# Reordering the first loads, with fewer warm-up matmuls, in a gated mix of memory attention and a GeGLU layer

## The chip, the core and the metric

The kernel runs on one core of a Trainium2 chip. Its engines are TensorE (PE: matmuls; PEld: the loads of their stationary operand), VectorE (DVE), ScalarE (ACT), GpSimd (POOL) and SyncE (SP), and each has a queue of its own that it works off in order. SyncE and ScalarE issue the DMAs. The metric is device time in microseconds (us) of one execution, the median of several. The profile is one further execution, taken by the hardware profiler; its times count from the first instruction, and lines such as L505 are lines of the kernel before.

## The reference

```
x = A_x                                               # 1 x 2048 x 512, bf16
g = sigmoid((x * gate_w).sum(-1, keepdims=True))
q, k, v = x @ wq, x @ wk, x @ wv                      # 32 heads of 16, 4 segments of 512
for s in range(4):
    p = softmax(q_s @ k_s.T * 16**-0.5 + mask)        # mask: ar[:, None] < ar[None, :]
    a_dot = p @ v_s
    a_mem = (phi(q_s) @ M) / (phi(q_s) @ z + 1e-6)
    o_s = sigmoid(beta) * a_mem + (1 - sigmoid(beta)) * a_dot
    M, z = M + phi(k_s).T @ v_s, z + phi(k_s).sum(rows)
a = concat(o) @ wo
b = (gelu(x @ w_gate) * (x @ w_up)) @ w_down          # 512 -> 1792 -> 512
return g * a + (1 - g) * b
```

Here phi(t) is t + 1 where t > 0 and exp(t) elsewhere. In the kernel the gate g is folded into factors, so that one accumulation per row tile holds both branches.

## The kernel before, in words

The four segments of 512 rows are worked one after another, but their tasks overlap. For a segment s, `prep` (L720) computes K, Q and V from the transposed input xT, `memory` (L826) the running M and z, `attention` (L860) the scores, their exponentials (ScalarE), masks (GpSimd) and value products; the gate, up and down matmuls of the GeGLU fill TensorE between the scores. Nearly all plain matmuls are recorded at L505 (128x128 stationary, up to 512 columns); the scores at L868 (four row tiles of 32) and the value products at L916 and L924 (column tiles) use the array in tiles.

Every piece of work is a task with a name. The order in which each engine works its tasks off is written out in `ORDER` (L41), one list for each engine; TensorE's pieces are named like `K0_1.2` (segment 0, tile 1, instruction 2 on). `schedule` (L240) goes through these lists with estimated durations and assigns the four PSUM banks; the constants `COLD` (L33: until when TensorE is taken to be at half speed) and `LANDING` (L37: when each early load is taken to have landed) enter it there (L281, L297). They issue nothing themselves. `Emitter` (L319) then writes each engine's stream, with a semaphore wait wherever a task reads what another engine or a DMA wrote.

The head of the program is what the change touches:

- ScalarE issues `wk` in two halves of 256 KB and then `wq` in two halves, and only then runs `tload` (L567), a one-column exponential that makes the table load happen early.
- SyncE issues the first segment's x in two halves of 256 rows (`x0_0`, `x0_1`, L572; they land in a part of hT[1]), then `wv` in two halves, half of `wg`, the second segment's x (transposing DMAs), `gate_w` (gwb), `beta` and the other half of `wg`.
- TensorE runs 11 warm-up matmuls on constants (L587: 512 columns, three of them 384), ten before and one behind the first transposes.
- Segment 0's x is transposed by TensorE (L599: x0t0a, x0t0b, x0t1 for the first half, x0t0, x0t1 for the second; eight transposes of 128 x 128 for each half) into PSUM, and copied out to xT by VectorE and ScalarE (x0ev..).
- The K projections of segment 0 (`proj_T`, L665) are cut into halves of 256 columns, one for each half of x0, each of four matmuls over the 128-row blocks kb. Matmul K0_t.j is block kb = j for the first half (j below 4) and kb = j - 4 for the second. `wk_of` (L675) says which load a block waits for: blocks 0 and 1 the first half of wk, blocks 2 and 3 the second.
- Q of segment 0 goes into the score banks X; V and the GeGLU gates into the four W banks.

The weights for up, down and out are loaded later, each behind the exponential of a given score group.

Of the kernel before, what the change touches and what calls it, by code (L numbers as in the profile page):

```python
# [32 lines left out]
COLD = 4.9  # L33
# [4 lines left out]
    "w_wk0": 4.8, "x0_0": 4.4, "w_wk1": 6.2, "x0_1": 5.8, "w_wq0": 8.2, "w_wv0": 7.4, "w_wq1": 10.1, "w_wv1": 8.9,  # L38
    "w_wg0": 11.5, "x1_0": 12.1, "w_gwb": 12.4, "x1_1": 13.0, "w_beta": 13.3, "x1_2": 13.8, "x1_3": 14.3,
# [3 lines left out]
        "warm0 warm1 warm2 warm3 warm4 warm5 warm6 warm7 warm8 warm9 x0t0a_0 x0t0b_0 x0t1_0 warm10 K0_0.0 K0_1.0 "  # L43
        "K0_2.0 K0_3.0 K0_0.1 K0_1.1 K0_2.1 K0_3.1 x0t0_1 x0t1_1 K0_0.2 K0_0.3 K0_2.2 K0_3.2 K0_2.3 K0_3.3 K0_1.2 "
        "K0_1.3 K0_1.4 K0_1.5 K0_1.6 K0_1.7 K0_3.4 K0_0.4 K0_0.5 K0_0.6 K0_0.7 K0_2.4 K0_3.5 Q0_1.0 K0_2.5 Q0_3.0 "
        "Q0_0.0 K0_2.6 K0_2.7 Q0_2.0 Q0_1.2 Q0_2.2 Q0_0.2 V0_1.0 Q0_3.2 V0_1.2 K0_3.6 V0_0.0 qk0_0A0 V0_3.0 "
        "K0_3.7 V0_3.2 V0_2.0 V0_0.2 V0_2.2 G1_1.0 qk0_0B0 G1_5.0 G0_4.0 G0_4.2 G0_5.0 G1_5.2 qk0_0L G0_8.0 "
        "G0_5.2 G0_8.2 G1_1.2 Q1_2.0 qk0_0A1 Q1_3.0 Q1_3.2 G0_3.0 G0_3.2 G1_2.0 qk0_0B1 G1_10.0 Q1_2.2 G1_10.2 "
        "G1_2.2 G1_11.0 G1_11.2 qk0_1A0 G0_1.0 G1_0.0 G0_1.2 G1_0.2 Q1_0.0 qk0_1B0 Q1_1.0 Q1_0.2 Q1_1.2 G1_9.0 "
        "G1_7.0 qk0_1A1 G1_9.2 K1_0.0 K1_0.2 G1_7.2 pv0_0_0 pv0_0_1 qk0_1B1 K1_1.0 G0_7.0 K1_1.2 G0_7.2 G0_9.0 "  # L50
        "G0_6.0 G0_9.2 qk0_2A0 G0_2.0 G0_6.2 K1_2.0 G0_2.2 K1_2.2 G0_10.0 qk0_2B0 G0_10.2 mz0 pv0_1_0 pv0_1_1 "
        "qk0_2L K1_3.0 G0_0.0 K1_3.2 V1_2.0 V1_0.0 qk0_2A1 G0_0.2 V1_2.2 G1_12.0 G1_12.2 V1_0.2 qk0_2B1 Q2_0.0 "
        "Q2_0.2 V1_3.0 G0_13.0 V1_3.2 qk0_3A0 G0_13.2 G1_6.0 G1_8.0 G1_8.2 G0_11.0 qk0_3B0 G0_11.2 G1_6.2 G1_3.0 "
        "G1_3.2 G1_4.0 qk0_3A1 G1_4.2 Q2_2.0 G0_12.0 G0_12.2 Q2_2.2 qk0_3B1 pv0_2_1 pv0_2_0 Q2_3.0 Q2_3.2 U0_1.0 "
        "G1_13.0 G1_13.2 V1_1.0 qk1_0A0 V1_1.2 U0_2.0 U0_1.2 U0_0.0 U0_0.2 U0_2.2 U0_3.0 U0_3.2 U0_4.0 U0_4.2 "
        "U0_9.0 U0_9.2 U0_7.0 U0_7.2 U0_10.0 U0_6.0 U0_10.2 U0_6.2 U0_8.0 U1_2.0 U0_8.2 U1_1.0 U1_2.2 U1_1.2 "
        "U1_5.0 U1_5.2 U1_7.0 U1_0.0 U1_0.2 U1_13.0 U1_13.2 num1_01.0 U1_7.2 U1_10.0 U1_10.2 pv0_3_1 pv0_3_0 "
        "qk1_0B0 U0_5.0 U0_5.2 U0_11.0 U1_6.0 U1_6.2 Q2_1.0 num1_00.0 qk1_0L U0_11.2 Q2_1.2 U1_11.0 U1_11.2 "
        "U0_13.0 qk1_0A1 D0_2.0 U0_12.0 U0_12.2 U0_13.2 D0_0.0 qk1_0B1 D0_0.2 D0_2.2 num1_02.0 D0_0.4 D0_0.6 "
        "U1_3.0 qk1_1A0 D0_0.8 D0_2.4 U1_3.2 U1_9.0 D0_2.6 U1_9.2 qk1_1B0 D0_2.8 D0_0.10 D0_0.12 D0_0.14 D0_0.16 "  # L60
        "num1_10.0 qk1_1A1 U1_8.0 U1_8.2 D0_2.10 D0_2.12 num1_11.0 D0_2.14 num1_12.0 qk1_1B1 U1_12.0 U1_12.2 "
        "D0_2.16 pv1_0_0 pv1_0_1 qk1_2A0 V2_3.0 K2_0.0 V2_3.2 K2_0.2 U1_4.0 qk1_2B0 U1_4.2 mz1 pv1_1_1 pv1_1_0 "
        "qk1_2L D0_1.0 D0_3.0 D0_3.2 D0_3.4 D0_1.2 qk1_2A1 D0_1.4 D0_1.6 D0_3.6 D0_1.8 D0_1.10 qk1_2B1 D0_1.12 "
        "V2_1.0 D0_1.14 K2_3.0 V2_1.2 qk1_3A0 D0_1.16 K2_3.2 K2_1.0 D0_3.8 K2_1.2 qk1_3B0 D0_3.10 D0_3.12 Q3_1.0 "
        "D0_3.14 Q3_1.2 qk1_3A1 V2_0.0 G2_0.0 K2_2.0 V2_0.2 K2_2.2 D0_3.16 qk1_3B1 pv1_2_0 pv1_2_1 G2_0.2 G2_1.0 "
        "G2_3.0 G2_1.2 G2_2.0 G2_3.2 G2_2.2 G2_4.0 G2_4.2 G2_6.0 G2_5.0 G2_5.2 G2_6.2 G2_7.0 G2_7.2 qk2_0A0 "
        "pv1_3_1 pv1_3_0 G2_8.0 G2_9.0 G2_8.2 G2_9.2 G2_11.0 G2_11.2 G2_10.0 G2_10.2 G2_12.0 G2_12.2 G2_13.0 "
        "G2_13.2 num2_00.0 U2_9.0 U2_9.2 U2_3.0 V2_2.0 D1_0.0 U2_3.2 V2_2.2 D1_0.2 D1_0.4 num2_01.0 D1_0.6 "
        "qk2_0B0 D1_0.8 U2_6.0 num2_02.0 D1_0.10 U2_6.2 U2_13.0 U2_13.2 qk2_0L D1_2.0 D1_0.12 Q3_0.0 Q3_0.2 "
        "D1_2.2 qk2_0A1 D1_2.4 U2_8.0 U2_8.2 D1_0.14 num2_11.0 D1_2.6 qk2_0B1 U2_10.0 D1_2.8 U2_10.2 D1_2.10 "  # L70
        "D1_0.16 num2_10.0 qk2_1A0 Q3_3.0 Q3_3.2 D1_2.12 D1_2.14 D1_2.16 num2_12.0 qk2_1B0 U2_0.0 U2_7.0 U2_0.2 "
        "Q3_2.0 U2_7.2 qk2_1A1 Q3_2.2 V3_0.0 V3_0.2 U2_4.0 U2_4.2 qk2_1B1 pv2_0_0 mz2 pv2_0_1 pv2_1_0 qk2_2A0 "
        "D1_1.0 D1_1.2 U2_11.0 U2_11.2 D1_1.4 qk2_2B0 U2_5.0 D1_1.6 D1_1.8 D1_1.10 pv2_1_1 qk2_2L D1_1.12 D1_1.14 "
        "U2_5.2 K3_3.0 K3_3.2 qk2_2A1 D1_3.0 D1_3.2 V3_2.0 D1_3.4 V3_2.2 qk2_2B1 D1_3.6 K3_2.0 K3_2.2 D1_1.16 "
        "K3_1.0 qk2_3A0 K3_1.2 D1_3.8 V3_1.0 D1_3.10 D1_3.12 qk2_3B0 U2_12.0 D1_3.14 D1_3.16 V3_1.2 U2_12.2 "
        "qk2_3A1 U2_1.0 V3_3.0 U2_1.2 pv2_2_0 pv2_2_1 qk2_3B1 V3_3.2 G3_0.0 G3_0.2 G3_1.0 K3_0.0 K3_0.2 G3_2.0 "
        "G3_2.2 G3_1.2 G3_5.0 G3_3.0 G3_3.2 G3_4.0 G3_4.2 G3_5.2 G3_7.0 G3_6.0 G3_6.2 G3_8.0 G3_7.2 G3_9.0 "
        "G3_10.0 G3_8.2 G3_9.2 G3_11.0 G3_10.2 G3_12.0 G3_11.2 G3_12.2 G3_13.0 G3_13.2 qk3_0A0 pv2_3_1 pv2_3_0 "
        "U3_9.0 U3_9.2 U2_2.0 U2_2.2 U3_8.0 U3_7.0 qk3_0B0 U3_5.0 U3_10.0 U3_8.2 U3_7.2 U3_5.2 qk3_0L U3_10.2 "
        "U3_3.0 U3_3.2 U3_4.0 D2_0.0 qk3_0A1 num3_01.0 U3_4.2 D2_0.2 D2_0.4 num3_00.0 D2_0.6 num3_02.0 qk3_0B1 "  # L80
        "D2_0.8 D2_0.10 D2_1.0 D2_1.2 U3_6.0 qk3_1A0 D2_0.12 U3_2.0 D2_0.14 U3_6.2 U3_2.2 qk3_1B0 D2_0.16 D2_1.4 "
        "U3_13.0 D2_1.6 D2_1.8 qk3_1A1 num3_11.0 num3_10.0 D2_1.10 D2_1.12 D2_1.14 U3_13.2 qk3_1B1 U3_1.0 "
        "num3_12.0 D2_1.16 U3_1.2 U3_0.0 qk3_2A0 pv3_0_0 pv3_0_1 U3_0.2 D2_3.0 qk3_2B0 D2_3.2 D2_3.4 pv3_1_1 "
        "pv3_1_0 qk3_2L D2_3.6 D2_3.8 D2_3.10 D2_2.0 D2_3.12 qk3_2A1 D2_3.14 D2_2.2 D2_2.4 D2_2.6 D2_3.16 qk3_2B1 "
        "D3_1.0 D2_2.8 D2_2.10 U3_12.0 U3_12.2 qk3_3A0 D3_1.2 D2_2.12 U3_11.0 D3_1.4 D2_2.14 qk3_3B0 U3_11.2 "
        "D3_0.0 D3_1.6 D2_2.16 D3_0.2 qk3_3A1 pv3_2_0 pv3_2_1 D3_1.8 D3_0.4 qk3_3B1 D3_0.6 D3_1.10 D3_0.8 D3_1.12 "
        "D3_0.10 D3_3w1.0 pv3_3_0 pv3_3_1 D3_3w0.0 D3_0.12 D3_2.0 D3_2.2 D3_0.14 D3_2.4 D3_2.6 D3_1.14 D3_0.16 "
        "D3_1.16 D3_3w1.4 D3_3w1.8 D3_3w0.4 D3_3w1.12 D3_3a1.0 D3_2.8 D3_2.10 D3_2.12 D3_2.14 D3_2.16 D3_3w0.8 "
        "D3_3w0.12 D3_3a0.0 "),
    "act": (  # L90
        "w_wk0 w_wk1 w_wq0 w_wq1 tload x0ev0b_0 x0ev1_0 K0_1ev K0_0even pke0_0 Q0_1ev Q0_0ev Q0_3ev gexp Vev0_1 "
        "exp0_0A0 Vev0_3 Vev0_0 exp0_0B0 gsum0_1 exp0_0L Gev1_1 exp0_0A1 gexs0 Gev0_3 exp0_0B1 pke0_1 exp0_1A0 "
        "Gev1_0 exp0_1B0 Q1_0ev exp0_1A1 pqe1_0 Gev1_9 exp0_1B1 K1_1ev Gev0_9 exp0_2A0 K1_2ev exp0_2B0 pqe1_1 "
        "exp0_2L K1_3ev exp0_2A1 Gev1_12 exp0_2B1 gsum1_0 exp0_3A0 Vev1_3 exp0_3B0 Gev1_3 exp0_3A1 Gev0_12 gexs1 "
        "exp0_3B1 gelu0_0 Gev1_13 gelu0_2 gelu0_6 gelu0_10 gelu1_0 gelu1_7 exp1_0A0 kl1_01 exp1_0B0 exp1_0L "
        "Q2_1ev exp1_0A1 exp1_0B1 pke1_0 exp1_1A0 pke1_1 exp1_1B0 fin0_0 exp1_1A1 pqe2_0 exp1_1B1 fin0_2 exp1_2A0 "
        "K2_0ev exp1_2B0 pqe2_1 exp1_2L exp1_2A1 exp1_2B1 gsum2_0 exp1_3A0 gsum2_2 exp1_3B0 gexs2 Q3_1ev exp1_3A1 "
        "K2_2ev exp1_3B1 gelu2_0 gelu2_1 gelu2_2 gelu2_3 gelu2_4 gelu2_5 gelu2_6 gelu2_7 gelu2_8 gelu2_9 gelu2_10 "
        "gelu2_11 gelu2_12 gelu2_13 exp2_0A0 exp2_0B0 pke2_0 exp2_0L exp2_0A1 pke2_1 exp2_0B1 fin1_0 exp2_1A0 "
        "Q3_3ev exp2_1B0 fin1_2 exp2_1A1 exp2_1B1 Vev3_0 exp2_2A0 exp2_2B0 pqe3_0 exp2_2L exp2_2A1 K3_3ev "  # L100
        "exp2_2B1 exp2_3A0 exp2_3B0 gsum3_3 gexs3 exp2_3A1 pqe3_1 exp2_3B1 gelu3_0 gelu3_1 gelu3_2 gelu3_3 "
        "gelu3_4 gelu3_5 gelu3_6 gelu3_7 gelu3_8 gelu3_9 gelu3_10 gelu3_11 gelu3_12 gelu3_13 exp3_0A0 exp3_0B0 "
        "exp3_0L exp3_0A1 exp3_0B1 exp3_1A0 exp3_1B0 exp3_1A1 exp3_1B1 exp3_2A0 exp3_2B0 exp3_2L exp3_2A1 "
        "exp3_2B1 fin2_3 exp3_3A0 exp3_3B0 exp3_3A1 exp3_3B1 fin3_0 fin3_1 fin3_2 fin3_30 "),
# [1079 lines left out]
```

## Time and profile before

| | us |
|---|---|
| median of 3 runs (266.59 to 267.54) | 267.41 |
| the profiled execution | 267.31 |
| its span, first to last instruction | 265.6 |
| TensorE busy in the span | 261.7 |
| ScalarE busy | 209.8 |
| VectorE busy | 201.2 |
| GpSimd busy | 109.0 |
| first warm-up matmul starts | 0.84 |
| first transpose of x0 starts | 5.10 |
| first K matmul starts | 5.88 |
| first scores start | 14.57 |

"Busy" counts an instruction from its start to its end. Matmuls are pipelined, so a busy TensorE may still have holes: what shows them is the distance from one matmul's start to the next. The time between the span and the measured time lies outside the first and last instruction. The chain that ended last is followed back from the end of the span, at each step to the work that released it. A landing time is counted from the start of a DMA's issue.

### The profile page before, as it was taken

To read this page: it belongs to the slowest core of one execution; us is meant where nothing else is said; L and a number is where in the kernel's file an instruction comes from. 1 tells how busy PE (TensorE), PEld (TensorE's weight loads), DVE (VectorE), ACT (ScalarE), POOL (GpSimd) and SP (SyncE) were. 2 spreads that over 40 slices of the span, in tenths; PEclk is the share of its full clock that TensorE was granted. 3 is DMA by queue.
4 is the path that set the end of the run, shared out by engine and by line. 5 is a ranking of instruction groups with operands and counts; after the bars stand their busy time and mean duration, and the time that the engine had idled before them with its cause. 6 is when DMAs were issued, how large, how long until landed. Compare 5 with 4: busy or idle time off the path is not lost.

```text
span 265.6 us, 7154 instructions
## 1 busy us (share of the span) xinstructions
PE 261.7 (99%) x3021; PEld 119.5 (45%) x3021; DVE 201.2 (76%) x399; ACT 209.8 (79%) x182; POOL 109.0 (41%) x256
## 2 busy tenths in 40 slices
PE   8999999999999999999999999999999999999995
PEld 3644345434445444534444444544444444444452
DVE  0589988989889897858987875886895965892650
ACT  3589998999997899979948798887977767768611
POOL 8305857075400483372560137416184056245400
PEclk9999999999999999999999999999999999999999
DMA  6960357905102443750000246200000202201002
GB/s 213 308 173 0 63 133 131 225 17 158 61 0 47 136 62 81 151 70 22 0 2 2 47 110 106 83 2 22 1 2 0 46 0 62 62 0 42 22 12 69
DMA packets 32752, 18.23 MB, mean 69 GB/s; under 512 B 20560, under 2 KB 32720, under 8 KB 32720
## 3 DMA queue, kind: packets, MB, share of 16 engines
q1 hardware_dynamic: 31632, 16.73, 27.4%
q10 hardware_dynamic: 1088, 1.05, 1.2%
q8 instruction: 23, 0.38, 0.6%
q14 instruction: 9, 0.07, 0.1%
HBM read 9.84 MB, written 2.10 MB: 45 GB/s over the span
## 4 chain that ended last, share of the span: by engine, by line
PE 96%; DMA 2%; ACT 1%; issue 0%; ACTq 0%
PE psW L505 76%; PE psXALL L868 9%; PE psW L916 6%; PE psXALL L505 3%; DMA hT<-in_A_x_dram 2%; PE psW L924 1%; PE psW L836 1%; ACT pt L874 1%; PE psXALL L599 0%; ACT ost L1044 0%; PE psW L590 0%; ACTq L401 0%
## 5 line engine op out<-in xcount | busy, mean ns | idle before, releaser
L874 ACT ACTIVATE pt<-psXALL 128x2048 bf16<-128x2048 f32 x64 | 120.1, 1876 | 23.3 <-PE psXALL L868 21.2
L877 POOL TENSOR_SCALAR_AFFINE_SELECT pt<-pt 128x256 bf16<-128x256 bf16 x128 | 57.5, 460 | 72.1 <-ACT pt L874 67.2
L505 PE MATMUL psW<-xT,wu 128*128 128x512 bf16 x224 | 56.0, 380 | 0.0
L505 PE MATMUL psW<-wd,hT 128*128 128x512 bf16 x210 | 55.2, 380 | 0.0
L505 PE MATMUL psW<-xT,wg 128*128 128x512 bf16 x224 | 53.4, 380 | 0.0
L877 POOL TENSOR_SCALAR_AFFINE_SELECT ptl<-ptl 128x512 bf16<-128x512 bf16 x32 | 23.9, 746 | 65.5 <-ACT ptl L874 63.8
L1015 DVE TENSOR_TENSOR hT<-psW,hT 128x512 bf16<-128x512 f32 x56 | 37.0, 682 | 14.3 <-PE psW L505 13.9
L505 PEld LDWEIGHTS psW<-xT,wg 128*128 128x128 bf16 x224 | 20.8, 98 | 25.7 <-issue 1.9
L505 PEld LDWEIGHTS psW<-xT,wu 128*128 128x128 bf16 x224 | 20.5, 98 | 24.7 <-issue 1.5
L930 DVE STREAM_TRANSPOSE tb<-psW 128x512 f32<-128x512 f32 x32 | 21.7, 701 | 9.0 <-PE psW L924 8.9
L505 PEld LDWEIGHTS psW<-wd,hT 128*128 128x128 bf16 x210 | 18.6, 98 | 21.6 <-issue 3.2
L868 PE MATMUL psXALL<-qT,kpad 32*128 32x320 bf16 (+3 forms) x512 | 25.4, 273 | 0.1
L999 ACT ACTIVATE hT<-psW 128x512 bf16<-128x512 f32 x28 | 15.4, 596 | 7.2 <-PE psW L505 7.1
L916 PE MATMUL psW<-pt,vaug 128*17 128x192 bf16 (+3 forms) x512 | 18.8, 273 | 0.0
L868 PEld LDWEIGHTS psXALL<-qT,kpad 32*128 32x128 bf16 x512 | 7.6, 92 | 23.9 <-ACT pt L874 14.2
L779 POOL COPY exsT<-exs 32x4 f32<-32x4 f32 x64 | 16.7, 261 | 3.7
L505 PE MATMUL psW<-wv,xT 128*128 128x512 bf16 x64 | 18.2, 380 | 0.0
L505 PE MATMUL psW<-xT,wk 128*128 128x512 bf16 (+1 forms) x80 | 18.0, 337 | 0.0
L874 ACT ACTIVATE ptl<-psXALL 128x2048 bf16<-128x2048 f32 x8 | 15.0, 1876 | 3.4 <-PE psXALL L868 3.4
L505 PE MATMUL psW<-wo,oT 128*128 128x512 bf16 x60 | 16.5, 381 | 0.0
L522 DVE CAST hT<-psW 128x512 bf16<-128x512 f32 x19 | 12.6, 682 | 2.2 <-PE psW L505 2.1
L916 PEld LDWEIGHTS psW<-pt,vaug 128*17 128x17 bf16 x512 | 10.6, 91 | 7.9 <-issue 3.2
(102 smaller groups left out, 311.2 us busy)
## 6 DMA issues: line engine op xcount, KB each, us to landing
out_dram<-ost SPq DMA_DIRECT2D x15, 128.0 KB, 1.7
wg<-in_B_w_gate_dram SPq DMA_DIRECT2D x2, 896.0 KB, 7.3
wu<-in_B_w_up_dram SPq DMA_DIRECT2D x2, 896.0 KB, 6.7
wd<-in_B_w_down_dram SPq DMA_DIRECT2D x2, 896.0 KB, 5.6
phkt<-in_A_x_dram SPq DMA_DIRECT2D x3, 512.0 KB, 5.4
vlow<-vaug SPq DMA_DIRECT2D x8, 136.0 KB, 2.7
hT<-in_A_x_dram SPq DMA_DIRECT2D x2, 256.0 KB, 4.7
wk<-in_A_wk_dram ACTq DMA_DIRECT2D x2, 256.0 KB, 5.1
```

The costliest lines, as they stand in the source:

```text
L505: return Instr(lambda e: e.matmul(view(), lhsT, rhs, start=first, stop=last), reads=reads, writes=[fkey if fkey is not None else g.key], e ...
L522: alts[DVE] = [Instr(lambda e: e.tensor_copy(dst(), src()), reads=reads, writes=writes, est=dve_t(n))]
L779: cross = task(f"exsT{s}", POOL, [Instr(lambda e, g=g, c=c: e.tensor_copy(exsT[sl][32 * g:32 * g + 32, c:16:4], exs[32 * c:32 * c + 32, s4 ...
L836: Instr(lambda e, t=t, kt=kt, c=c: e.matmul(gm.f32()[32 * c:32 * c + 32, 34 * t:34 * t + 34].rearrange("p (j e) -> p j e", e=17), phkt[:, ...
L868: instrs.append(Instr(lambda e, g=g, lhs=lhs, rhs=rhs, c0=c0, ncol=ncol: e.matmul(X[g][:, c0:c0 + ncol], lhs(32 * g), rhs(32 * g), start=T ...
L874: exp_task(s, f"exp{s}_{t}{name}", [Instr(lambda e: e.activation(dst[:], XALL[:, :].rearrange("p (g c) -> p g c", g=4), ACTF.Exp, scale=AT ...
L877: task(f"msk{s}_{t}{name}", POOL, [Instr(lambda e, view=view, pat=pat, base=base: e.affine_select(out=view, in_=view, compare_op=ALU.is_ge ...
L916: instrs.append(Instr(lambda e, t=t, q=q, kb=kb, slot=slot, c0=c0: e.matmul(gp.f32()[32 * q:32 * q + 17, 128 * kb + 64:512], Vaug[sl][:, k ...
L924: instrs.append(Instr(lambda e, t=t, q=q, kb=kb, c0=c0: e.matmul(gp.f32()[32 * q:32 * q + 17, 128 * kb:128 * kb + 64], Vlow[j][:, kb, 4 * ...
L930: task(f"pvt{s}_{t}_{j}", DVE, [Instr(lambda e: e.transpose(Tb[:, j, :], gp.f32()[:, :]), [gp.key], [("Tb", j)], dve_t(512))], grp=gp)
L999: lambda e, g=g, ft=ft, s=s: e.activation(hT[s % 2][:, ft, :], g.f32()[:, :], ACTF.Gelu_apprx_tanh),
L1015: task(f"Um{s}_{ft}", DVE, [Instr(lambda e, g=g, ft=ft: e.tensor_tensor(hT[sl][:, ft, :], g.f32()[:, :], hT[sl][:, ft, :], ALU.mult), [g.k ...
```

## The change

ScalarE's queue begins with `tload`; its DMAs come behind it. `wk` comes in three pieces (128 KB, 128 KB, 256 KB) and is followed, behind the first eviction of x0, by `wv`. `wq` moves to SyncE's queue, behind x0, into the place that `wv` had. The number of warm-ups falls from 11 to 7, the last of 256 columns, and all of them stand ahead of the transposes. On TensorE all 16 transposes of x0 now come before the first K matmul. The five lists of `ORDER` are new from end to end, with other choices, too, of which of ScalarE and VectorE copies a result out; the first parts of four of them are shown. `COLD` and `LANDING` take other values, which act only through `schedule`.

```diff
-COLD = 4.9
+COLD = 4.4
...
 ORDER = {
     "pe": (
-        "warm0 warm1 warm2 warm3 warm4 warm5 warm6 warm7 warm8 warm9 x0t0a_0 x0t0b_0 x0t1_0 warm10 K0_0.0 K0_1.0 "
-        "K0_2.0 K0_3.0 K0_0.1 K0_1.1 K0_2.1 K0_3.1 x0t0_1 x0t1_1 K0_0.2 K0_0.3 K0_2.2 K0_3.2 K0_2.3 K0_3.3 K0_1.2 "
-        "K0_1.3 K0_1.4 K0_1.5 K0_1.6 K0_1.7 K0_3.4 K0_0.4 K0_0.5 K0_0.6 K0_0.7 K0_2.4 K0_3.5 Q0_1.0 K0_2.5 Q0_3.0 "
...
+        "warm0 warm1 warm2 warm3 warm4 warm5 warm6 x0t0a_0 x0t0b_0 x0t1_0 x0t0_1 x0t1_1 K0_1.0 K0_2.0 K0_3.0 "
+        "K0_3.1 K0_0.0 K0_1.1 K0_0.1 K0_2.1 K0_1.2 K0_0.2 K0_3.2 K0_1.3 K0_0.3 K0_0.4 K0_0.5 K0_1.4 K0_0.6 K0_1.5 "
+        "K0_2.2 K0_1.6 K0_0.7 K0_3.3 K0_1.7 K0_2.3 Q0_2.0 K0_3.4 K0_3.5 K0_3.6 K0_3.7 Q0_0.0 Q0_3.0 Q0_0.2 Q0_2.2 "
+        "Q0_3.2 Q0_1.0 Q0_1.2 G0_2.0 G0_2.2 G0_1.0 qk0_0A0 G0_1.2 K0_2.4 V0_0.0 V0_0.2 V0_2.0 V0_2.2 qk0_0B0 "
...
     "act": (
-        "w_wk0 w_wk1 w_wq0 w_wq1 tload x0ev0b_0 x0ev1_0 K0_1ev K0_0even pke0_0 Q0_1ev Q0_0ev Q0_3ev gexp Vev0_1 "
...
+        "tload w_wk0 w_wk1 w_wk2 x0ev1_0 w_wv0 w_wv1 x0ev1_1 K0_0even K0_0ev K0_3ev pke0_0 Q0_0ev Q0_2ev Q0_1ev "
...
     "dve": (
-        "x0ev0a_0 x0ev0_1 x0ev1_1 kl0_11 K0_0ev kp0_1 K0_2ev Q0_2ev kl0_10 kl0_01 gmul0 gsum0_0 K0_3ev kl0_21 "
...
+        "x0ev0a_0 x0ev0b_0 x0ev0_1 K0_1ev kl0_11 kl0_10 kp0_0 kl0_00 kp0_1 kp0_3 Q0_3ev gmul0 kl0_30 kl0_31 "
...
     "sp": (
-        "x0_0 x0_1 w_wv0 w_wv1 w_wg0 x1_0 w_gwb x1_1 w_beta x1_2 x1_3 w_wg1 pkT0_1 Vlo0_0 pkT0_0 Vlo0_1 pkT0_2 "
...
+        "x0_0 x0_1 w_wq0 w_wq1 w_wg0 x1_0 w_gwb x1_1 w_beta x1_2 x1_3 w_wg1 pkT0_1 Vlo0_1 Vlo0_0 w_wu0 pkT0_2 "
...
+    wloads = [(wkey, i, w[:, k0:k1, :], r4(src)[:, k0:k1, :])
+              for wkey, w, src, cuts in (("wk", wk, A_wk, (0, 1, 2, 4)), ("wq", wq, A_wq, (0, 2, 4)),
+                                         ("wv", wv, A_wv, (0, 2, 4)))
+              for i, (k0, k1) in enumerate(zip(cuts, cuts[1:]))]
     for u in range(2):
...
-        wdma(("wk", u), ACT, wk[:, 2 * u:2 * u + 2, :], r4(A_wk)[:, 2 * u:2 * u + 2, :], (220000, 310000)[u], issue=0.45)
-    for key, w, src, e in (("wq", wq, A_wq, ACT), ("wv", wv, A_wv, SP)):
-        for i in range(2):
-            wdma((key, i), e, w[:, 2 * i:2 * i + 2, :], r4(src)[:, 2 * i:2 * i + 2, :], 250000, issue=0.46)
+        for wkey, i, dst, src in wloads[u:u + 1] if u == 0 else wloads[1:]:
+            wdma((wkey, i), SP if wkey == "wq" else ACT, dst, src, 250000, issue=0.5)
...
-    for i in range(11):
+    for i in range(7):
         gw = Grp(banks)
-        n = 384 if i in (6, 9, 10) else 512
+        n = 256 if i == 6 else 512
...
-        wk_of = lambda kb: ("w", (wkey, kb // 2))
+        wk_of = lambda kb: ("w", (wkey, min(kb, 2) if wkey == "wk" else kb // 2))
```

## The prediction

> **What bounds the kernel now.** I read the page first (busy shares and the chain that ended last), then the timeline of the first 16 us, the landing times of the first loads, and last the spacing of TensorE's matmuls over the whole span.
>
> ```profile
> span 265.6 us, 7154 instructions
> ...
> PE 261.7 (99%) x3021; PEld 119.5 (45%) x3021; DVE 201.2 (76%) x399; ACT 209.8 (79%) x182; POOL 109.0 (41%) x256
> ...
> PE 96%; DMA 2%; ACT 1%; issue 0%; ACTq 0%
> ```
>
> TensorE is the bound from end to end: 96% of the chain is its own work. The 2% of DMA is the wait for x0's first half at the start. So a change gains only where real work starts sooner or where holes between matmuls close. The head, by the timeline (start, duration, engine, line, out<-in, count):
>
> ```profile
> 0.81 0.97 SPq L536 DMA_DIRECT2D hT<-in_A_x_dram  x2
> 0.81 1.03 ACTq L536 DMA_DIRECT2D wk<-in_A_wk_dram  x2
> ...
> 0.84 4.21 PE L590 MATMUL psW<-const-bfloat16-1.0 128*128 128x512 bf16 x10 [0.84 <-PEq L1169]
> ...
> 2.91 1.28 ACT L567 ACT_TABLE_LOAD   x1 [2.91 <-issue]
> ...
> 4.20 0.20 ACT L567 ACTIVATE stmp<-const-bfloat16-1.0 128x1 f32<-128x1 bf16 x1
> ...
> 5.10 0.76 PE L599 MATMUL psXALL<-ident,hT 128*128 128x128 bf16 x8
> ...
> 5.70 0.33 PE L590 MATMUL psW<-const-bfloat16-1.0 128*128 128x384 bf16 x1
> ...
> 5.88 1.05 PE L505 MATMUL psW<-xT,wk 128*128 128x256 bf16 x8
> ...
> 6.77 0.61 PE L599 MATMUL psXALL<-ident,hT 128*128 128x128 bf16 x8
> ...
> 7.22 2.24 PE L505 MATMUL psW<-xT,wk 128*128 128x256 bf16 x19
> ```
>
> Ten warm-ups cover the wait; the first transposes start at 5.10, and from there TensorE waits for no load: each row starts where the issue of the one before ended (8 matmuls of 256 columns from 5.88 to 6.77 are 0.11 each, 8 transposes from 6.77 to 7.22 are 0.056 each). The first 8 transposes took 0.60 (5.10 to 5.70), 0.15 more than the second 8, since the array still ran at half speed (warm-ups of 512 columns start 0.43 apart, later matmuls of that size 0.216). The eleventh warm-up took 0.18. So the real work stands as if it had run at full speed without warm-ups from 5.10 + 0.15 + 0.18 = **5.43**. This "start" S is what I compare.
>
> Behind the head the trace has one hole of size, at score matmuls that waited for an exponential (226.25 to 228.13):
>
> ```profile
> 227.04 1.03 PE L505 MATMUL psW<-xT,wu 128*128 128x512 bf16 x4
> 228.18 0.40 PE L868 MATMUL psXALL<-qT,kpad 32*128 32x448 bf16 x8
> ```
>
> Four matmuls from 227.04 are issued by 227.04 + 4 x 0.216 = 227.90, then 0.28 passes, where 0.10 is usual: 0.18 lost. The usual 0.10 is the change from plain matmuls to the tiled ones of scores and values (two plain ones from 14.04 are issued by 14.47; scores start at 14.57). The way back costs 0.09.
>
> **The change part by part.** The dropped warm-ups filled a wait. The 7 kept take 6 x 0.43 + 0.21 = 2.8, from 0.84 to 3.6 in place of 5.05. Only the eleventh lay on the path; its 0.18 is inside S.
>
> **x0.** Its halves stay first and second on SyncE's queue, issued at 0.81 and 1.32. They landed at 5.06 (0.81 + 4.25, from the chain) and 6.4, while wk's halves landed at 5.4 and 6.9. The second halves, with us to landing last:
>
> ```profile
> wk<-in_A_wk_dram ACTq DMA_DIRECT2D x1, 256.0 KB, 5.6
> hT<-in_A_x_dram SPq DMA_DIRECT2D x1, 256.0 KB, 5.1
> ```
>
> and the rows by half microsecond, with GB/s last, show the path full from 3.0 on:
>
> ```profile
> 2.50:3.00 0.50, 0.50 (x3) 0.22 (x2) 0.00 (x0) 0.09 (x1) 0.50 (x2) 1.00 0.64 147
> 3.00:3.50 0.50, 0.50 (x3) 0.22 (x2) 0.00 (x0) 0.50 (x1) 0.50 (x3) 1.00 1.06 371
> ```
>
> So 512 KB had landed by 5.4 and 1 MB by 6.9: 1.5 for 512 KB. If x0 has the path to itself, its second half lands when x0's first and wk's first half together did, at 5.4; if wk shares as before, at 6.4. I take the middle, 5.9. All 16 transposes now stand ahead of the first K matmul; the first 8 (at half speed 0.85, from about 4.7) end by then, so only the last 8 follow the landing: S = landing + 0.05 (5.06 to 5.10 before) - 8 x 0.056 = landing - 0.40 = 5.5, between 5.0 and 6.0.
>
> **wk.** It comes in three pieces (128, 128, 256 KB) behind the table load and its activation. Three issues of 0.5 follow them, and nothing on ScalarE is due before the transposes, so the issues hide. What counts is the last piece: ahead of the first K matmul that needs it stand 16 transposes (0.89) and 8 K matmuls (0.87), so S = landing + 0.05 - 1.76. Without delay it lands as wk's second half did, 6.9: S = 5.2. With the whole of table load and activation in front, 1.49, at 8.4: S = 6.7. In the rows a transfer issued at 0.81 shows little movement before 2.5, so part of an issue's lateness is spent in a start-up that the full path hid anyway; and ScalarE's next issue can leave at 2.1 (0.81 + 1.28), still ahead of the full path at 3.0. I take the lower part, 7.2: S = 5.5. The pieces before it are needed less early and bind later.
>
> **Other loads.** wq takes wv's place on SyncE's queue, same sizes; its first K-deep pair has 16 transposes and 24 K matmuls (3.5) ahead, against a landing near 8 before: S = 4.6, no bound. wg's first half landed at 2.84 + 9.4 = 12.2 and is now first used behind 16 transposes, 28 K and 8 Q matmul pairs (0.89 + 3.05 + 3.46 = 7.4): S = 4.9. It doesn't bind, but it caps any gain at 0.5. wv is issued behind x0's first ScalarE eviction, about 5.5, and holds ScalarE's queue for two issues (1.0); the eviction behind it is then ready near 7.1, and the K matmul that reads it comes 16 matmuls behind the first, near 7.7: hidden by 0.6. With that cover gone it costs up to 0.5.
>
> S = 5.5 against 5.43: **+0.07**, between -0.4 and +1.25.
>
> **Orders.** I counted changes of tile mode in the two lists of TensorE: 160 before, 163 after (some value groups and a memory product, which earlier stood beside other tiled work, now stand alone). 3 x 0.095 = **+0.28**. Between scores and the next ones ScalarE needs 0.53 (225.72 to 226.25) + 1.88 + 0.05 = 2.46; the slot that was short (eight plain matmuls and two small ones) now holds ten plain ones, and no new slot is shorter than 2.46 by the same addition: **-0.18**, with 0 to +0.5 for up to three slots that I mis-added. VectorE's wait for gate_w (landed at 13.3) now comes before some score-side copies, but the scores that read them are some 5 us later. Eight TensorE instructions fewer shift its code blocks, whose loads stop nothing in this trace: 0.
>
> **Tail.** The last eviction (0.58) and store are the same. The third tile's eviction goes to VectorE, 0.68 beside the six matmuls of 0.16 that still follow: 0, at most 0.1.
>
> Sum on the profiled execution: span 265.6 within 267.31 measured, +0.07 + 0.28 - 0.18 = +0.17, so **267.5**. The median of the three runs, 267.41, stands 0.1 above it, their spread is 0.95; about 0.5% (1.3 us) is what a measurement of this kernel can tell from no change.
>
> **Rivals.**
>
> *Loads at their best* (0.17): x0 alone on the path, wk undelayed: S = 5.2, sum -0.13 to -0.2, 267.1. For it: the path was full when both shared. Against: wk is issued 1.3 later.
>
> *wk behind the table load* (0.11): the delay is paid in full, S = 6.7: +1.25 + 0.28 - 0.18, 268.7. It decides once wk's last piece lands after 7.2, and each microsecond later costs one. For it: TABLE_LOAD is 1.28 and nothing else would move wk.
>
> *Half speed lasts longer* (0.12): slower. Full speed came at about 5.4, after 4.6 of unbroken matmuls. Now TensorE idles from 3.6 to about 4.7 and again until 5.9. If the count starts again with the transposes, full speed comes at 4.7 + 4.6 = 9.3, and the real work from 6.0 on runs at half speed for 3.3: it loses 1.65, 269.1. It decides if the first K matmuls start 0.21 apart in place of 0.11. Against it: a good part of the time is still busy. The granted clock reads 1.00 throughout the head, so it can't tell. The Trainium skill ("TensorE: Matmul & The Clock Gate", Part 1: The HAM clock gate) says that the gate opens after a busy window of about 3.4 us whose phase the kernel doesn't set; by that rule a window that misses costs until the next one, 5.4 + 3.4 = 8.8, an estimate of 1.4 us. The trace agrees that the change comes after some 4 us of matmuls, and shows nothing on gaps.
>
> *More than the loads can give* (0.05): over 1.3 faster would need S below 4.1, before x0's first half lands even at its best; wg forbids it. Only the spread of the runs (0.7 below the profiled one) on top of the best case comes near.
>
> The forecast itself holds 0.55. Range: the best case with part of the runs' spread below, 266.6; the late wk above, 268.7. Chances: slower by over 0.5% takes the half-speed rival and half of the late wk (0.18); faster 0.06; the rest 0.76 is within.
>
> **What would show it.** Right: K's first matmul near 6.4, 0.11 apart, no gap before the ninth; x0's second half landed near 5.9; 163 mode changes; no hole over 0.1 behind 14 us. Wrong: wk's last piece after 7.5, K matmuls 0.21 apart, score matmuls waiting for ScalarE in stage 0.

## The result, and the profile after

Slower by 0.7%: 269.49 us median (9 runs, 267.9 to 269.75) against 267.27 (9 runs); ratio 1.007, 95% interval 1.0046 to 1.0093. The nine runs are no single cloud: three lie at 267.9 to 268.17, six at 269.4 to 269.75, and nothing between. Two things have to be explained, then: why even the lower group (middle run 268.05) is 0.8 above the time before, and what the 1.5 between the groups is. The profiled execution (268.17) is one of the lower group.

Its page, with the lines that answer to those of before:

```profile
span 266.1 us, 7100 instructions
...
PE 255.9 (96%) x2977; PEld 118.3 (44%) x3017; DVE 203.8 (77%) x402; ACT 208.2 (78%) x180; POOL 105.0 (39%) x256
...
PE 92%; issue 2%; DVE 2%; DMA 2%; ACT 1%; SPq 0%; ACTq 0%
```

TensorE's share of the chain fell from 96% to 92%: VectorE, not named in the line of before, is now in it with 2%. (Of TensorE's busy time read only the chain: 40 matmul records are missing here, 2977 matmuls against 3017 weight loads.) The head, from the timeline (start, duration, engine, line, operation, count, idle time before):

```profile
0.81 1.28 ACT L567 ACT_TABLE_LOAD   x1 [0.81 <-PEq L1171]
0.81 0.97 SPq L536 DMA_DIRECT2D hT<-in_A_x_dram  x2
...
0.84 2.93 PE L592 MATMUL psW<-const-bfloat16-1.0 128*128 128x512 bf16 x7 [0.84 <-PEq L1171]
0.87 1.45 ACTq L536 DMA_DIRECT2D wk<-in_A_wk_dram  x3
...
4.32 0.62 PE L601 MATMUL psXALL<-ident,hT 128*128 128x128 bf16 x8 [0.54 <-DMA hT<-in_A_x_dram]
...
5.61 0.62 PE L601 MATMUL psXALL<-ident,hT 128*128 128x128 bf16 x8 [0.67 <-DMA hT<-in_A_x_dram]
...
6.06 2.80 PE L505 MATMUL psW<-xT,wk 128*128 128x256 bf16 x24
```

Three readings. wk's three issues leave between 0.87 and 2.32, while the table load runs (0.81 to 2.09), so it holds them back by no more than 0.06 (the first left at 0.81 before). x0's second half lands at 5.56 and wk's last piece at 6.82. And the array is at full speed from the first transpose on: 8 transposes start 0.056 apart, 24 K matmuls 0.11 apart. This execution's start S is 5.17, 0.26 better than before's 5.43. From S to the start of the last matmul ("the rest" below) it takes 257.75, where before took 256.94. So against that one profile the head won 0.26, and the part behind the head lost 0.81. (The 0.26 is no measure of the loads: x0's first half landed at 5.06 in that profile, and at 4.30 to 4.44 in all five later profiles with the old loads; more on this below.)

Where that part loses is seen at 54 to 59 us, in the same timeline:

```profile
53.69 2.12 POOL L879 TENSOR_SCALAR_AFFINE_SELECT ptl<-ptl 128x512 bf16<-128x512 bf16 x3
...
54.55 2.31 DVE L852 TENSOR_TENSOR mzbd<-mzacc,gbd 32x136 bf16<-32x136 f32 x4
...
54.73 1.88 ACT L876 ACTIVATE pt<-psXALL 128x2048 bf16<-128x2048 f32 x1 [0.60 <-POOL ptl L879]
...
56.67 0.40 PE L870 MATMUL psXALL<-qT,kpad 32*128 32x320 bf16 x8 [0.17 <-ACT pt L876]
...
56.88 0.69 DVE L769 TENSOR_REDUCE glog<-phkt 128x1 f32<-128x512 bf16 x1
...
57.49 0.68 DVE L522 CAST hT<-psW 128x512 bf16<-128x512 f32 x1
...
58.23 1.04 PE L505 MATMUL psW<-xT,wg 128*128 128x512 bf16 x4 [0.19 <-DVE hT L522]
```

The scores at 56.67 wait for an exponential that starts late: by the distance of matmul starts 0.24 is lost. The view puts the 0.60 that ScalarE was idle before it down to GpSimd's mask, but the trace's semaphores say otherwise. The mask's signal came at 54.36, the semaphore instruction in front of the exponential ended at 54.38, and the exponential began only 0.35 after that, at 54.73; in the profile of before the same step took 0.04 (54.55 to 54.60). The plain matmuls at 58.23 need a PSUM bank that VectorE empties at 57.49 to 58.17, because a product of four small instructions (2.31) and a sum (0.69) stand ahead of that copy: 0.36 lost. A third hole, behind the matmul at 115.7, is 0.04. Before's hole of 0.18 at 228 is gone. The changes of tile mode are three more, as counted (+0.28). Two of the three memory products, which had stood behind plain matmuls, now stand behind value products and behind scores, and their 64 matmuls take 0.633 and 0.583 from first start to last where they took 0.528 (+0.16). 0.64 - 0.18 + 0.28 + 0.16 = 0.90, against 0.81 measured: 0.09 too much, which stays open.

For the lower group this nearly closes the sum: 267.31 - 0.26 + 0.81 = 267.86, and it lies at 267.9 to 268.17. (What lies outside the span differs between executions: 1.7 before, 2.0 in this one.) The profile on record says nothing of the upper group. That is what the experiments begin with.

### The profile page after: what moved, and what is told of

It is laid out like the page before. It is cut to its first block, busy times and chain, and to the rows that moved or that the text cites. A ratio compares the mean times of both kernels' runs of the same rounds, so it can differ in the third digit from the quotient of the medians.

```text
span 266.1 us, 7100 instructions
## 1 busy us (share of the span) xinstructions
PE 255.9 (96%) x2977; PEld 118.3 (44%) x3017; DVE 203.8 (77%) x402; ACT 208.2 (78%) x180; POOL 105.0 (39%) x256
## 3 DMA queue, kind: packets, MB, share of 16 engines
q10 hardware_dynamic: 1104, 1.05, 1.2%
## 4 chain that ended last, share of the span: by engine, by line
PE 92%; issue 2%; DVE 2%; DMA 2%; ACT 1%; SPq 0%; ACTq 0%
PE psW L505 73%; PE psXALL L870 9%; PE psW L918 6%; PE psXALL L505 3%; DMA hT<-in_A_x_dram 2%; PE psW L926 1%; ACT pt L876 1%; DVE mzbd L852 1%; PE psW L838 0%; DVE tb L932 0%; DVE vaug L522 0%; DVE glog L769 0%; PE psXALL L601 0%; DVE hT L522 0%; ACT ost L1063 0%
## 5 line engine op out<-in xcount | busy, mean ns | idle before, releaser
L879 POOL TENSOR_SCALAR_AFFINE_SELECT pt<-pt 128x256 bf16<-128x256 bf16 x128 | 55.4, 443 | 137.7 <-ACT pt L876 132.8
L505 PE MATMUL psW<-xT,wu 128*128 128x512 bf16 x213 | 55.4, 380 | 1.2 <-issue 0.8
L505 PE MATMUL psW<-wd,hT 128*128 128x512 bf16 x200 | 53.7, 380 | 1.4 <-issue 1.1
L505 PE MATMUL psW<-xT,wg 128*128 128x512 bf16 x215 | 51.9, 379 | 1.4 <-issue 0.6
L879 POOL TENSOR_SCALAR_AFFINE_SELECT ptl<-ptl 128x512 bf16<-128x512 bf16 x32 | 23.3, 729 | 1.7
L522 DVE CAST hT<-psW 128x512 bf16<-128x512 f32 x22 | 14.8, 686 | 4.2 <-PE psW L505 4.1
L781 POOL COPY exsT<-exs 32x4 f32<-32x4 f32 x64 | 15.7, 245 | 6.0 <-ACT exs L772 2.3
L505 PE MATMUL psW<-xT,wk 128*128 128x512 bf16 (+1 forms) x78 | 17.4, 336 | 0.3 <-issue 0.3
L505 PE MATMUL psW<-wv,xT 128*128 128x512 bf16 x62 | 17.1, 380 | 0.2 <-issue 0.2
```

Of the source, the lines that this page charges most:

```text
L505: return Instr(lambda e: e.matmul(view(), lhsT, rhs, start=first, stop=last), reads=reads, writes=[fkey if fkey is not None else g.key], e ...
L522: alts[DVE] = [Instr(lambda e: e.tensor_copy(dst(), src()), reads=reads, writes=writes, est=dve_t(n))]
L781: cross = task(f"exsT{s}", POOL, [Instr(lambda e, g=g, c=c: e.tensor_copy(exsT[sl][32 * g:32 * g + 32, c:16:4], exs[32 * c:32 * c + 32, s4 ...
L879: task(f"msk{s}_{t}{name}", POOL, [Instr(lambda e, view=view, pat=pat, base=base: e.affine_select(out=view, in_=view, compare_op=ALU.is_ge ...
```

## The experiments

**Theories.** On the groups: theory 1, the idle stretch that the dropped warm-ups leave lets the array stay at half speed for some 3.5 us more in some executions, but not in all; theory 2, x0 or wk lands late in some executions. On the 0.81: theory A, it is the new orders' own; theory B, the orders are as good as the old ones, and the moved loads make them late. (Where the expectations speak of theory 3, they mean that the loss sits behind the head.) "Ten warm-ups" below are eight of 512 columns and two of 384, as in the kernel before without the eleventh. All ratios are to the kernel before on the same chip: 267.22 and 267.23 median in the first two sets of runs, 267.0 in the last.

**The changed kernel again.** No edit.

> The changed kernel once more, nothing altered. Its nine times fell into two groups, three at 267.9 to 268.2 and six at 269.4 to 269.8; the profiled execution was of the lower one. Theory 1 (half speed): the groups differ in when TensorE comes to full speed. Then both groups show again, some 1.5 us apart, and a profile that falls into the upper group shows K's matmuls of 256 columns 0.21 us apart in place of 0.11 for about 3 us. Theory 2 (landing): the upper group is executions whose first loads land some 1.5 us later; such a profile shows TensorE waiting for x0 or wk and no matmul 0.21 apart. Theory 3 (orders): the loss sits behind the head; such a profile has the head of the lower group and more holes behind 14 us.

Measured: 269.45; four runs at 267.86 to 268.0, five at 269.45 to 270.15; ratio 1.0057 (1.0025 to 1.009). This profile fell into the upper group (269.76). Its head, TensorE in the timeline:

```profile
0.84 2.93 PE L592 MATMUL psW<-const-bfloat16-1.0 128*128 128x512 bf16 x7 [0.84 <-PEq L1171]
...
4.37 1.03 PE L601 MATMUL psXALL<-ident,hT 128*128 128x128 bf16 x8 [0.59 <-DMA hT<-in_A_x_dram]
...
5.66 1.03 PE L601 MATMUL psXALL<-ident,hT 128*128 128x128 bf16 x8 [0.26 <-DMA hT<-in_A_x_dram]
...
6.49 3.73 PE L505 MATMUL psW<-xT,wk 128*128 128x256 bf16 x20
```

x0 lands as in the other profile (second half at 5.61), and wk's last piece, later at 7.49, is still ahead of the ninth K matmul (8.19) that needs it. The first transposes start within 0.05 of the other profile's, but 8 transposes take 1.03 in place of 0.62, and K matmuls start 0.213 apart until 9.3, 0.109 after that. S is 6.98, 1.81 more; the rest is 257.81, the same. Theory 1 is shown here in one trace, and 267.31 - 0.26 + 0.81 + 1.81 = 269.67 lies within the upper group. The granted clock in the rows by time reads 1.00 through this head too, because the rows print 1.00 wherever the trace has no clock record. The record, which no view lists by time, does tell: in this trace it begins, at full clock, at 9.31; in the profile of the lower group at 3.91; in that of before at 5.44. In each of the 11 traces that have one it begins where the spacing halves, or in a pause of the matmuls just before.

**The kernel before with 7 warm-ups.** Nothing else of the change.

```diff
-    for i in range(11):
+    for i in range(7):
-        n = 384 if i in (6, 9, 10) else 512
+        n = 256 if i == 6 else 512
```

> The kernel before with seven warm-ups as in the changed one (six of 512 columns, one of 256, all ahead of the transposes), nothing else; the gap it opens is from 3.8 to 5.1. Theory 1: some runs 1 to 2 us above the kernel before, others up to 0.2 below it (the warm-up behind the transposes is gone). Theory 2 and theory 3: all runs at 267.1 to 267.5, as before.

Measured: 267.15; seven runs at 266.56 to 267.43, five at 268.35 to 269.16; ratio 1.0014 (0.999 to 1.0037). So dropping warm-ups alone, with the old loads and orders, goes with two groups. This rests on the shares, as none of the five was profiled: of the 69 runs of the kernel before in all sets, three, of the same set, lie as high (268.50 to 269.03), and what they lost isn't known. The profile is of the lower group:

```profile
4.43 0.89 PE L601 MATMUL psXALL<-ident,hT 128*128 128x128 bf16 x8 [0.66 <-DMA hT<-in_A_x_dram]
5.21 1.05 PE L507 MATMUL psW<-xT,wk 128*128 128x256 bf16 x8
```

The first transposes end at half speed, K is at full speed from its first matmul, and S is 4.78. That is 0.65 better than in the profile of before, most of it because x0's first half landed at 4.38 in place of 5.06; beside the ten warm-ups below, with x0 at 4.30, it is 0.43.

**The kernel before with 3 warm-ups.** As above, with `range(3)`, all of 512 columns.

> The kernel before with three warm-ups of 512 columns in place of eleven, nothing else: TensorE is idle from about 2.1 until x0 lands (4.4 to 5.1). Theory 1 (idle time puts off full speed): all or nearly all runs in the upper group, 268.3 to 269.2, and the profile shows K's matmuls of 256 columns 0.21 apart for 2 us or more. Theory 2 (the groups come from the landing of the loads): the same two groups in the same shares as with seven warm-ups, 266.6 to 267.4 in half of the runs or more.

Measured: 268.51 (6 runs, 267.96 to 269.15); ratio 1.0052 (1.0033 to 1.007). The lower group is gone.

```profile
4.49 1.04 PE L601 MATMUL psXALL<-ident,hT 128*128 128x128 bf16 x8 [2.20 <-DMA hT<-in_A_x_dram]
...
5.31 1.92 PE L507 MATMUL psW<-xT,wk 128*128 128x256 bf16 x8
...
7.02 1.06 PE L601 MATMUL psXALL<-ident,hT 128*128 128x128 bf16 x8
```

x0 arrives as with seven, and 8 K matmuls take 1.92 where they took 1.05; 0.11 apart they are only from 9.0, where the clock record begins (8.98). Nothing else was changed, so theory 2 falls as the cause of the groups.

**The kernel before with 10, and with 9 warm-ups.** `range(10)` with the old widths; and eight of 512 columns and one of 256, which end 0.4 earlier, about where x0 can land.

> The kernel before without its eleventh warm-up. It stood between the transposes and K and took 0.18 there. Theory 1: 0.1 to 0.2 below before, 267.0 to 267.1, spread as before. Theory 2: the same.

> The kernel before with nine warm-ups (eight of 512 columns, one of 256, ending at 4.5, about where x0 lands in three of the four last profiles), none behind the transposes. Theory 1: the 0.5 that ten warm-ups hold x0 back is won and TensorE is hardly idle, so one group at 266.6 to 266.9, below before. Theory 2: two groups as with seven warm-ups, 266.6 to 266.9 and 268.4 to 269.2.

Measured: 267.1 (12 runs, 266.64 to 267.5), ratio 0.9998 (0.9985 to 1.0011); and 267.09 (12 runs, 266.62 to 267.48), ratio 0.9996 (0.9983 to 1.0009). Neither has an upper group, and neither differs from the kernel before; the second misses its expectation of 266.6 to 266.9. In the second, TensorE never rests from 0.84 on, and still the change of speed came only at 6.4:

```profile
4.42 1.06 PE L601 MATMUL psXALL<-ident,hT 128*128 128x128 bf16 x8
5.28 1.58 PE L507 MATMUL psW<-xT,wk 128*128 128x256 bf16 x8
6.69 0.61 PE L601 MATMUL psXALL<-ident,hT 128*128 128x128 bf16 x8
```

So the eleventh warm-up's 0.18 can't be told from nothing in the time, and what unbroken matmuls buy is not an early change of speed: in the eight profiles that have them it comes anywhere from 3.9 to 6.4, and in none of them later.

**The changed kernel with 10 warm-ups.** This takes the half speed out of the change and leaves loads and orders.

```diff
-    for i in range(7):
+    for i in range(10):
-        n = 256 if i == 6 else 512
+        n = 384 if i in (6, 9) else 512
```

> The changed kernel with ten warm-ups ahead of the transposes, of the sizes before, in place of seven; nothing else. They end at 5.05, ahead of the landing of x0's second half (5.56 in the profile). Theory 1: the upper group goes, all runs at 267.9 to 268.3, about 1.4 us below the changed kernel's median. Theory 2 and theory 3: both groups stay, median 269.4.

Measured: 268.22 (8 runs; seven at 267.89 to 268.83, one at 270.45); ratio 1.0041 (1.0024 to 1.0057). The upper group is gone, 1.2 of the loss with it, and the 1.0 that is left is loads and orders. The profile fell on the one outlier, which has a cause of its own:

```profile
6.04 1.04 PE L508 MATMUL psW<-xT,wk 128*128 128x256 bf16 x8
...
8.58 1.69 PE L508 MATMUL psW<-xT,wk 128*128 128x256 bf16 x14 [1.51 <-DMA wk<-in_A_wk_dram]
```

The ninth K matmul waits for wk's last piece, landed at 8.45 in place of 6.8: 1.67 lost. That is the prediction's late wk, once, and not because of the table load, since the issues left at the same times as in the other profiles. The rest is 257.82 without it.

**New loads with old orders, and old loads with new orders,** both with 10 warm-ups. In the first, the five lists are those of before, with only `tload`, the load names and the transposes of x0 placed as in the change; in the second, the queues of SyncE and ScalarE and wk's halves are those of before, and all else in the lists is new.

> The changed kernel's loads and transposes-first head with ten warm-ups, and behind the head the orders of the kernel before. Theory 1 with the sum from the two traces (head 0.26 sooner, orders 0.8 later): 266.9 to 267.1, one group, 0.2 to 0.4 below before. Theory 3 (the loads give nothing, the orders take all): 267.3. Theory 2: two groups, as in the changed kernel.

> The changed kernel's orders (transposes first too) on the loads of before, with ten warm-ups that end at 4.9. The holes and mode changes of the new orders cost 0.8 from K on in every profile of them so far. Theory 3 in this form (0.8 fixed): 267.9 to 268.2, and the hole pair near 57 us shows again. If the holes come from the new loads instead (they show in one profile of the old orders too, 0.24 at 56.4): 267.2, no hole pair.

Measured, new loads: 268.49 (9 runs, 267.47 to 269.31), ratio 1.005 (1.0032 to 1.0069), missing its expectation. Its profile (267.79) shows half speed until 6.1. Its rest is 257.37, with a hole of 0.12 at 13.3 where V matmuls wait for wv, which is issued later now, before's 0.18 at 228, and 0.24 at 56.4, so that hole comes with the old orders too:

```profile
55.03 1.88 ACT L878 ACTIVATE pt<-psXALL 128x2048 bf16<-128x2048 f32 x1 [0.48 <-POOL pt L881]
...
56.97 0.40 PE L872 MATMUL psXALL<-qT,kpad 32*128 32x320 bf16 x8 [0.17 <-ACT pt L878]
```

Here, too, the exponential begins 0.35 after the semaphore instruction in front of it, which ended at 54.68. (A mask's signal at 54.92 lies between, so in this one profile the mask isn't excluded.) All six profiles with the new loads have this late start (0.35 each) and this hole; none of the six with the old loads has either. In the six this exponential is the 64th record of ScalarE's queue in the trace, in the others the 63rd: the new loads put one more DMA issue ahead of it. So this hole came with the moved loads; why the 64th record is late isn't shown. The median stands 0.70 above the profiled run, and what the slower runs lost isn't shown either. Measured, new orders: 268.32 (6 runs, 268.16 to 268.51), ratio 1.0042 (1.0026 to 1.0059), rest 257.79; it was expected at 267.9 to 268.2. With the loads of before, the hole behind VectorE's product stands in the same place, and is larger (0.59):

```profile
55.08 2.30 DVE L853 TENSOR_TENSOR mzbd<-mzacc,gbd 32x136 bf16<-32x136 f32 x4
...
58.75 1.04 PE L508 MATMUL psW<-xT,wg 128*128 128x512 bf16 x4 [0.42 <-DVE hT L525]
```

Theory A holds: 257.79 against the 256.92 and 256.94 of the profiles with old loads and old orders is 0.87 that the new orders lose by themselves. Theory B has a part, too: moved loads cost old orders 0.45. The two don't add up. In the new orders wv's 0.12 doesn't show, and the two waits near 57 stand one behind the other: 0.24 and 0.36 with the new loads, 0.59 in one without them.

**VectorE's product moved,** in the changed kernel with 10 warm-ups: once behind Q2_0's eviction, once five places further.

```diff
-        "gmul1 Gev1_12 Vev1_0 mzbd0 gsum1_1 Gev0_13 K1_3ev Q2_0ev gsum1_2 pvt0_2_1 Gev1_8 pvt0_2_0 Gev0_0 gts1 "
+        "gmul1 Gev1_12 Vev1_0 gsum1_1 Gev0_13 K1_3ev Q2_0ev mzbd0 gsum1_2 pvt0_2_1 Gev1_8 pvt0_2_0 Gev0_0 gts1 "
```

> The changed kernel with 10 warm-ups, and in VectorE's order the product mzbd0 (2.31 for its four small instructions) moved from ahead of a sum, two evictions' places back, to behind Q2_0's eviction. Theory (the hole of 0.36 near 57.7 to 59.3 comes from a PSUM bank that VectorE frees late, behind this mzbd0): that hole shrinks below 0.1, everything else stays, so 0.26 to 0.36 under the 268.2 of the changed kernel with 10 warm-ups: 267.9. Rival (VectorE is simply late there as a whole, and a later eviction then frees its bank late instead): the hole moves or stays, sum of holes within 0.1 of before, 268.2.

> As the run beside it, with mzbd0 moved four places further, behind the eviction Gev0_0. Theory: the hole of 0.36 is gone as well, 267.9; since mzbd0 is then ready later, the memory product of the next segment that reads it could wait, and a new hole of up to 2 would show there. Rival: the hole stays or moves among the plain matmuls near 57 to 60, 268.2.

Measured: 268.18 (6 runs, 267.86 to 268.89), ratio 1.0044 (1.0028 to 1.0059); and 268.08 (8 runs, 267.98 to 269.84), ratio 1.0055 (1.0035 to 1.0075). Both were expected at 267.9. The times decide nothing, neither between the two nor against 268.22: the intervals are 0.8 and more wide. The traces do. Behind Q2_0:

```profile
57.51 0.59 PE L508 MATMUL psW<-xT,wk 128*128 128x512 bf16 x2
57.94 1.03 PE L508 MATMUL psW<-xT,wg 128*128 128x512 bf16 x4
```

The matmuls follow on without a wait, the hole of 0.36 is gone and nothing has taken its place: the rest is 257.39, 0.43 less. Five places further, it is gone as well, but the work that VectorE was kept from comes late at another place, 0.40 at 66.0:

```profile
66.61 0.60 PE L508 MATMUL psW<-xT,wu 128*128 128x512 bf16 x2 [0.24 <-DVE qT L525]
```

and the rest is 257.79 again. So that hole's cause is shown by traces, and the hole at 56.2, which has another cause (ScalarE's late start), stays in both at 0.24. No version here is faster than the kernel before by more than its interval.

All heads side by side ("full speed" is where the trace's clock record begins and the spacing of matmuls halves; S includes what half speed costs real work):

| profile | TensorE idle ahead of transposes | full speed at | S | rest |
|---|---|---|---|---|
| before | 0.05 | 5.4 | 5.43 | 256.94 |
| before, 10 warm-ups | no | 5.3 | 5.21 | 256.92 |
| before, 9 | no | 6.4 | 5.37 | 256.92 |
| new loads, old orders, 10 | no | 6.1 | 5.46 | 257.37 |
| old loads, new orders, 10 | no | 6.4 (by spacing; no record) | 5.72 | 257.79 |
| changed, 10 | no | 4.5 | 5.15 (and the 1.67) | 257.82 |
| changed, 10, product behind Q2_0 | no | 4.2 | 5.24 | 257.39 |
| changed, 10, five places further | no | 3.9 | 5.27 | 257.79 |
| changed, 7 (lower) | 0.54 | 3.9 | 5.17 | 257.75 |
| changed, 7 (upper) | 0.59 | 9.3 | 6.98 | 257.81 |
| before, 7 (lower) | 0.66 | 5.0 | 4.78 | 256.92 |
| before, 3 | 2.20 | 9.0 | 6.66 | 256.92 |

For 9 and 3 warm-ups, S is the last matmul's start less the rest that the other runs with old orders have; counted from the matmuls of the head it comes to the same within 0.01.

## Why the prediction was wrong

- **The step that failed: "The dropped warm-ups filled a wait."** I priced them at nothing but the eleventh's 0.18. They kept the array busy until the change of speed, and without them it comes 3.5 to 4 later than in before in part of the executions: 1.81 between the two profiles of the changed kernel, and 11 of its 18 runs lie in the upper group. I had written this down as a rival and given it 0.12, with 1.65 as its price and full speed at 9.3; measured were 1.81 and 9.3. The argument against it, that a good part of the time was still busy, holds only for the other 7 runs. What I should have read as a warning is that before had only 0.05 of idle time ahead of its transposes, so its profile couldn't show what more of it costs. Nor was the granted clock of 1.00 in its first rows a reading: the trace has no clock record ahead of 5.44.
- The rival's mechanism was half right. A count that starts again with the transposes would come out the same in every run; the same program gave 3.9 and 9.3. The Trainium skill ("TensorE: Matmul & The Clock Gate", Part 1: The HAM clock gate) says that the gate watches a free-running window of about 3.4 us, whose phase differs from run to run. These traces agree: the stretch at full clock lasts 259.413 in seven of them and 262.826 in four, which is 76 and 77 times 3.413; unbroken matmuls from 0.84 give 3.9 to 6.4, and programs that missed a window got 9.0 or 9.3; the 8.8 worked out by that rule was near.
- How much idle time such a stretch bears can be bounded by laying 3.41 back from the start of the clock record. The one that brought full speed to the kernel before with 7 warm-ups (1.63 to 5.04) held 0.65 of idle time. In the upper profile of the changed kernel the record begins at 9.31, so the stretch before the last was 2.49 to 5.90; it held 0.59 + 0.26 = 0.85 and brought none. An estimate from these two: the bound lies between 0.65 and 0.85. In the lower profile of the changed kernel such a stretch ended at 3.91, before most of the idle time. By this reading it was where the stretch fell, and not 0.54 against 0.59, that parted the two profiles.
- **Orders: +0.28 - 0.18 forecast, +0.81 measured.** The three mode changes and the vanished hole came as counted. What was missing are holes of 0.24 and 0.36 and the memory products' 0.16. I had checked the slots of scores against ScalarE's 2.46, but not which evictions stand behind VectorE's small products, where the 0.36 sits. The 0.24 was in no term: I had looked at what the instruction count shifts on TensorE, but not on ScalarE, whose 64th record starts 0.35 late with the moved loads. The forecast's own test, no hole over 0.1 behind 14 us, failed behind the matmuls at 56.1 and 57.7.
- **wk behind the table load: assumed wrong, result harmless.** I let the issues leave at 2.1; they leave from 0.87, during the load. The last piece lands at 6.82, not 7.2. The one run with 8.45 shows that this step can bind, as its formula said: 8.45 - 1.71 = 6.74, measured 5.15 + 1.67 = 6.82.
- **x0: the landing right, the gain not.** Second half at 5.56 and 5.61, between the bounds 5.4 and 6.4 and nearer the good end; S = 5.56 - 0.40 = 5.16, measured 5.17. Transposes of the second half bound the start, as worked out. But the 5.43 that this was set against is of an execution in which x0's first half landed late, at 5.06; that the one profile of before was such a one is luck. In the later profiles with old loads it landed at 4.30 to 4.44, and S is 5.21 with ten warm-ups and 4.78 with seven. Beside them the changed head wins nothing (5.15 to 5.27 with ten, 5.17 with seven): x0's second half does land sooner (5.5 to 5.65 against 5.7 to 6.0), but with all transposes first the K matmuls wait for it. And wk's last piece lands later (6.8 to 8.45 against 6.1 to 6.3).
- wq, wg and the tail cost nothing, and VectorE's wait for gate_w made no hole: right. The wait for wv was hidden in the new orders, and showed as 0.12 when the old ones were put beside the new loads.

## What to carry to other kernels

Price a warm-up by the speed of the work behind it, not by the wait that it fills: an idle stretch before the array has reached full speed can cost one more window of half speed, and it does so in some runs only, so one profile can't tell; look at the spread of the times, at the start-to-start distance of matmuls and at where the trace's clock record begins. When the order of work is rebuilt, look on every engine that frees a bank for the longest small work ahead of an eviction, not only at the engine that was nearly the bound. And before a gain is counted against one profile, see whether its loads landed where they usually do.

## What the runs showed of the hardware

- The spacing of matmuls halves at 3.9 to 6.4 with unbroken work from 0.84 (eight profiles); with idle stretches at 3.9, 5.0, 9.0 or 9.3. The trace's clock record begins at the same moment; the rows by time print 1.00 before it, too.
- An exponential that is the 64th record of ScalarE's queue started 0.35 after the end of the semaphore instruction in front of it, in all six profiles where it stood there (median of such steps in the same traces: 0.045). Why is open.
- ScalarE's DMA issues go out while its table load runs (issues at 0.87, 1.31 and 1.83, load from 0.81 to 2.09), and the activation behind it starts at 2.10.
- The same transfers, issued at the same times, can land 1.6 apart (wk's last 256 KB at 6.82 and 8.45).
- Four VectorE products of 32 x 136 took 2.31, 2.30, 1.51 or 1.29, depending on where they stood; what slows them was not tried.
